# Seven on-chip transposes moved from TensorE to DMA, unread warm-up matmuls, and a new order of loads

## Chip, cores, metric

One core of one Trainium2 chip. The metric is device time in microseconds of one execution, slowest (here only) core; lower is better. A profiled execution also has a span, from its first to its last instruction, which is 1.7 to 2.0 us shorter than that run's time. Ratios are the mean time of one kernel's fast runs over the mean of the other's fast runs of the same rounds, so they are not quite the ratio of the medians quoted beside them. A run more than 1.5% above the fastest of its kernel counts as slow, not fast; medians and ranges below are over all runs, and slow runs are named.

## The reference

Packed attention for 8 batches of 8 heads, then a bilinear feed-forward network; all inputs are random.

```python
p_packed = sm_attn(p, k, v)          # p: 8 x 8 x 32 x 64;  q, k, v: 8 x 8 x 576 x 64
out = sm_attn(q, p_packed, p_packed) # softmax attention, scale 1/8
x = out.transpose(0, 2, 1, 3).reshape(8 * 576, 512)
return ((x @ w1) * (x @ w2)) @ w3 @ w_out   # w1, w2: 512 x 1024; w3: 1024 x 1024; w_out: 1024 x 512
```

## The kernel before

A Python scheduler runs at build time. Each operation has a duration, buffers that it reads and writes, and a wanted time made from tuned constants (`CONF`); a list scheduler with a cost model fixes one order for each engine. On the chip every engine then works through its queue in that order. These parts matter here (cuts marked):

```python
# loads: all on GpSimd's software queue, float32 in HBM cast to float16 on the way;
# two buffers each for k, v and q, used by even and odd batches
def load_in(which, b):
    ...
    env.nc.gpsimd.dma_start(out=t[0:SC, :, :], in_=x[b].rearrange("h (p c) d -> p h (c d)", c=CK))

# a "turn": k or q of one batch, 96 x 3072, transposed on TensorE through PSUM
for g in range(2):
    ps = Psum(2)
    for u in range(2):
        ...   # 6 transposes of 96 x 128 each, 24 in all           (L412)
    ...       # copy PSUM -> kT or qT, on VectorE or ScalarE         (L425, L427)

# va: v is copied into another layout by VectorE                    (L433)
# s1, pv, s2, z: the two attentions (L445, L468, L514, L534)
# fold: w3 @ w_out, once for all (L347 transposes w3, L365 multiplies)
# G: packed values times w1, w2 (L557); gate: a2 times G (L585)
# ab: product of the two gate halves, VectorE, frees the gate's PSUM (L601)
# project: ab times the folded weight (L624); o: copy out; st: store, on SP's queue
```

The softmax here doesn't subtract the row's maximum and nothing guards it: scores larger than these inputs give would overflow.

## Time and profile before

| | before |
|---|---|
| median of the runs beside the changed kernel | 213.82 us (212.99 to 214.01, 4 runs) |
| span of the profiled run | 212.7 us |
| TensorE work, counts times start-to-start durations | 187.9 us |
| TensorE not at work before the turn of q1 | 17.6 us |
| TensorE waiting after it | 1.8 us |
| last matmul's end to the end of the span | 5.3 us |

The turn of q1 is a mark that stands after the same amount of TensorE work, 34.9 us, in both kernels. I got waits by laying the durations that the prediction lists along TensorE's order and subtracting them from the intervals between starts; the prediction, which used rounder numbers, had 2.0 and 5.2 for the last two rows.

### The profile page before, as it was taken

To read this page: it belongs to the slowest core of one execution; us is meant where nothing else is said; L and a number is where in the kernel's file an instruction comes from. 1 tells how busy PE (TensorE), PEld (TensorE's weight loads), DVE (VectorE), ACT (ScalarE), POOL (GpSimd) and SP (SyncE) were. 2 spreads that over 40 slices of the span, in tenths; PEclk is the share of its full clock that TensorE was granted. 3 is DMA by queue.
4 is the path that set the end of the run, shared out by engine and by line. 5 is a ranking of instruction groups with operands and counts; after the bars stand their busy time and mean duration, and the time that the engine had idled before them with its cause. 6 is when DMAs were issued, how large, how long until landed. Compare 5 with 4: busy or idle time off the path is not lost.

```text
span 212.7 us, 6124 instructions
## 1 busy us (share of the span) xinstructions
PE 195.0 (92%) x2656; PEld 131.5 (62%) x2656; DVE 116.0 (55%) x188; ACT 137.0 (64%) x209; POOL 32.9 (15%) x49
## 2 busy tenths in 40 slices
PE   0188989999999999999999999999999999999990
PEld 0168878667567748785457766757755646776440
DVE  4015434367867776587946845447485665555100
ACT  2154749865798476986899555797858567555321
POOL 7742245511131112111000000100000000000000
PEclk9999999999999999999999999999999999999997
DMA  5999999999999999999829203192013313103353
GB/s 68 185 193 202 206 203 200 197 203 204 205 241 230 224 204 249 203 212 205 177 53 150 62 0 103 49 167 80 20 23 82 99 52 99 54 13 86 99 151 101
DMA packets 34124, 29.51 MB, mean 139 GB/s; under 512 B 3888, under 2 KB 28464, under 8 KB 34096
## 3 DMA queue, kind: packets, MB, share of 16 engines
q0 software_dynamic: 28336, 19.66, 62.7%
q1 hardware_dynamic: 5760, 9.44, 15.4%
q8 instruction: 21, 0.34, 0.6%
q14 instruction: 7, 0.06, 0.1%
HBM read 39.32 MB, written 9.44 MB: 229 GB/s over the span
## 4 chain that ended last, share of the span: by engine, by line
PE 89%; DMA 3%; ACT 2%; DVE 2%; issue 1%; POOL 0%; DVEq 0%; ACTq 0%; POOLq 0%
PE ps L585 29%; PE pb L624 29%; PE pb L365 8%; PE ps L412 7%; PE ps L557 5%; DMA ab<-in_moe_w_dram 3%; PE pb L445 2%; PE pb L468 2%; PE ps L534 2%; PE ps L624 2%; PE ps L514 2%; PE pb L347 1%; ACT ab L357 1%; PE ps L445 1%; DVE pT L334 1%
## 5 line engine op out<-in xcount | busy, mean ns | idle before, releaser
L585 PE MATMUL ps<-a,G 128*128 128x288 f16 x512 | 70.8, 286 | 0.2
L624 PE MATMUL pb<-wc,ab 128*128 128x512 bf16 x272 | 68.7, 380 | 0.0
L601 DVE TENSOR_TENSOR ab<-ps,bs 128x576 bf16<-128x576 f32 x64 | 48.2, 755 | 30.7 <-ACT bs L597 25.1
L585 PEld LDWEIGHTS <-G 128*128 128x128 f16 x512 | 48.5, 98 | 17.0 <-issue 0.9
L597 ACT CAST bs<-ps 128x576 bf16<-128x576 f32 x64 | 40.9, 639 | 26.5 <-PE ps L585 26.0
L624 PEld LDWEIGHTS <-ab 128*128 128x128 bf16 x288 | 25.8, 98 | 25.1 <-issue 2.7
L572 ACT CAST G<-ps 128x1024 f16<-128x1024 f32 x20 | 19.8, 1015 | 4.6 <-PE ps L557 4.4
L637 DVE COPY o<-pb 128x512 f32<-128x512 f32 x15 | 10.4, 691 | 20.7 <-PE pb L624 11.0
L639 ACT COPY o<-pb 128x512 f32<-128x512 f32 x19 | 11.1, 585 | 15.3 <-PE pb L624 15.0
L365 PE MATMUL pb<-wo,ab 128*128 128x256 f16 x128 | 16.7, 286 | 2.3 <-ACT ab L357 1.4
L570 DVE CAST G<-ps 128x1024 f16<-128x1024 f32 x12 | 14.4, 1221 | 3.2 <-PE ps L557 2.9
L365 PEld LDWEIGHTS <-ab 128*128 128x128 f16 x128 | 12.5, 102 | 5.2 <-ACT ab L357 2.7
L347 PE MATMUL pb<-ident,ab 128*128 128x128 f16 x48 | 4.8, 266 | 9.0 <-DMA ab<-in_moe_w_dram 9.0
L278 POOL DMA_DIRECT2D qin<-in_q_dram x8 | 6.2, 772 | 40.2 <-PE ps L412 34.2
L427 ACT COPY qT<-ps 128x1152 f16<-128x1152 f16 x9 | 10.0, 1117 | 3.4 <-PE ps L412 3.2
L540 ACT ACTIVATE ln<-ps 128x576 f32<-128x576 f32 x16 | 10.1, 650 | 2.7 <-PE ps L534 2.5
L557 PE MATMUL ps<-w,ppT 64*32 64x256 f16 x512 | 10.9, 272 | 0.1
L544 ACT ACTIVATE ri<-ln 128x576 f16<-128x576 f32 x16 | 10.7, 687 | 0.3
L456 ACT ACTIVATE es<-pb 96x512 f16<-96x512 f32 x18 | 10.4, 594 | 0.6
L347 PEld LDWEIGHTS <-ab 128*128 128x128 f16 x64 | 4.9, 116 | 9.4 <-DMA ab<-in_moe_w_dram 9.0
L357 ACT COPY ab<-pb 128x1024 f16<-128x1024 f16 x5 | 5.0, 1016 | 8.5 <-PE pb L347 8.5
L412 PE MATMUL ps<-ident,kin 96*128 96x96 f16 x192 | 10.3, 206 | 0.0
(56 smaller groups left out, 185.1 us busy)
## 6 DMA issues: line engine op xcount, KB each, us to landing
kin<-in_k_dram POOLq DMA_DIRECT2D x8, 576.0 KB, 13.6
vin<-in_v_dram POOLq DMA_DIRECT2D x8, 576.0 KB, 15.5
qin<-in_q_dram POOLq DMA_DIRECT2D x8, 576.0 KB, 15.5
out_dram<-o SPq DMA_DIRECT2D x24, 192.0 KB, 2.5
out_dram<-o SPq DMA_DIRECT2D x24, 128.0 KB, 2.4
ab<-in_moe_w_dram POOLq DMA_DIRECT2D x8, 256.0 KB, 10.2
w<-in_moe_w_dram POOLq DMA_DIRECT2D x8, 256.0 KB, 12.2
out_dram<-o SPq DMA_DIRECT2D x24, 64.0 KB, 2.2
```

Of the source, the lines that this page charges most:

```text
L347: env.nc.tensor.transpose(t[:, 128 * ct : 128 * ct + 128], env.w3[:, ci, 128 * ct : 128 * ct + 128], env.ident[:, :])
L365: env.nc.tensor.matmul(pv(ps)[:, 0:256], env.w3T[:, ci, 128 * ct : 128 * ct + 128], env.wo[:, h, ct, :], start=(ct == 0), stop=(ct == DFC ...
L412: env.nc.tensor.transpose(t[:, u, SC * hc : SC * hc + SC], s[0:SC, h, 128 * c3 : 128 * c3 + 128], env.ident[0:SC, 0:SC],)
L544: env.nc.scalar.activation(out=env.ri[g][:, :, :], in_=env.ln[g][:, :, :], func=AF.Exp, scale=-1.0)
L557: env.nc.tensor.matmul(pv(ps)[32 * hp : 32 * hp + 32, g, 256 * w : 256 * w + 256], env.ppT[b % 2][64 * g : 64 * g + 64, g, 32 * hp : 32 * ...
L570: env.nc.vector.tensor_copy(o, pv(ps))
L572: env.nc.scalar.copy(out=o, in_=pv(ps))
L585: env.nc.tensor.matmul(pv(ps)[:, half, 0:HS], env.G[b % 2][:, mc // 2, g, w, 128 * (mc % 2) : 128 * (mc % 2) + 128], env.a2[b % 2][:, g, h ...
L597: env.nc.scalar.copy(out=env.bs[bs][:, :, :], in_=pv(ps)[:, :, 0:HS])
L601: env.nc.vector.tensor_mul(env.ab(pair)[:, mc, b % 2, :].rearrange("p (a s) -> p a s", a=2), pv(ps)[:, :, 0:HS], env.bs[bs][:, :, :],)
L624: env.nc.tensor.matmul(pv(ps), ab[:, ic, 128 * t : 128 * t + 128], env.wc[:, ic, :], start=(ic == 0), stop=(ic == DFC - 1),)
L639: env.nc.scalar.copy(out=env.o[ob][:, :], in_=pv(ps))
```

## The change

Its intent: take seven of the sixteen turns off TensorE and give them to the DMA engines' transpose; let loads pause meanwhile (the code's reason for it is "transposes apart from loads"); keep TensorE's clock up from the start with matmuls that nobody reads; and rebuild the scheduler's model of the DMA queue and tune all orders again. Core of the diff:

```diff
 CONF = dict(
-    dma_from=8,
+    turn="q4 q6 k4 k7 q7 q5 k6",
+    order="q3 v2 k4 k2 k3 q4 v5 q5 v4 q2 k5 v3 Tk4 Tq4 Tq5 k7 Tk7 k6 v6 q6 Tk6 Tq6 v7 q7 Tq7",
+    warm=True,
     ...   # all other constants tuned again
-    loads="wo0 w33 w37 w36 pp w30 k_0 w34 wo1 v_0 q_0 w31 w35 k_1 ww0 w32 ww1 ww3 ww2 v_1 q_1",
+    loads="w34 w32 wo0 k_0 w31 w36 w30 pp wo1 k_1 v_0 w33 q_0 w35 w37 ww0 ww1 ww3 ww2 v_1 q_1",
@@ consts: the constant that unread matmuls read is set first
-        nc.vector.memset(env.pT[:, :, :, :], 0.0)
         nc.vector.memset(env.blk[:, :], 0.0)
         ...
+        nc.vector.memset(env.pT[:, :, :, :], 0.0)
@@ attention
-            if by_dma:
+            if f"{which}{b}" in conf["turn"]:
                 def fn(e):
                     ...
-                    env.nc.sync.dma_start_transpose(
+                    return env.nc.sync.dma_start_transpose(
                         out=t[:, 0 : 24 * SC].rearrange("p (j r) -> p j r", j=24),
                         in_=s[0:SC, :, :].rearrange("p h x -> p (h x)"),
                     )
@@ after the plan: loads and transposes wait for each other, group by group
+        op.gates = list(gate_on)
+    def fill(e):
+        for i in range(8):
+            env.nc.tensor.matmul(pv(fill.ps)[:, 0:128], env.blk[:, :], env.blk[:, :], start=True, stop=True)
@@ emission
+        if op.name == "fill":
+            ...
+            for p in getattr(op, "gates", ()):
+                tc.add_manual_dep(made[op].ins, made[p].ins.name, ..., reason="transposes apart from loads")
 (cut: class Dma, the model of the queue, used only to choose the order)
```

More of the change, by code (lines that the diff above doesn't have):

```diff
@@ L22 @@
 CONF = dict(
-    dma_from=8,
-    P=25.15,
-    T0=59.57,
-    lead=1.32,
-    at=dict(kT=-0.8, va=-0.14, s1=0.87, pv=0.59, ppT=-0.87, qT=-0.07, s2=0.43, z=0.51, G=0.14),
-    G_w=-0.01,
-    tg=[-30.99, -12.45, -0.15, 8.05, -11.49, -2.63, 7.81, -7.38, -17.47, 4.27],
-    ta=[-60.59, -5.81, -1.16, 6.18, -17.56, 4.69, -5.65, -11.68],
-    proj_off=0.87,
-    proj_w=0.98,
-    gate_w=0.03,
-    loads="wo0 w33 w37 w36 pp w30 k_0 w34 wo1 v_0 q_0 w31 w35 k_1 ww0 w32 ww1 ww3 ww2 v_1 q_1",
-    fold0=57.8,
-    fold1=3.02,
-    fold_w=3.51,
+    turn="q4 q6 k4 k7 q7 q5 k6",
+    order="q3 v2 k4 k2 k3 q4 v5 q5 v4 q2 k5 v3 Tk4 Tq4 Tq5 k7 Tk7 k6 v6 q6 Tk6 Tq6 v7 q7 Tq7",
+    warm=True,
+    P=29.2291,
+    T0=80.6499,
+    lead=1.3115,
+    at=dict(kT=-1.6236, va=0.0107, s1=0.7618, pv=0.4288, ppT=-1.4299, qT=-1.2631, s2=-1.2122, z=0.5004, G=0.2508),
+    G_w=-0.1978,
+    tg=[-23.1099, -3.311, 10.4569, -2.7587, 6.032, 9.5469, -1.2936, -11.1124, -14.9496, 8.7305],
+    ta=[-46.4062, -60.559, 5.856, -5.9212, -20.778, -0.73, -27.3654, -33.788],
+    proj_off=2.8077,
+    proj_w=1.1912,
+    gate_w=0.0325,
+    loads="w34 w32 wo0 k_0 w31 w36 w30 pp wo1 k_1 v_0 w33 q_0 w35 w37 ww0 ww1 ww3 ww2 v_1 q_1",
+    fold0=107.041,
+    fold1=-16.2447,
+    fold_w=5.6366,
 )
@@ L100, with __init__, run @@
 OVERLAP = {"ACT": 0.10, "DVE": 0.083}
-BEGIN, DMA_BEGIN, LAG = 1.27, 2.6, 0.6
+BEGIN, DMA_BEGIN = 1.27, 2.6
+FILL, FILL_END, WARM_AT = 0.44, 20.0, 6.5
+class Dma:
+    def __init__(self, scale=1.0):
+        self.free, self.scale, self.rest = DMA_BEGIN, scale, 0.0
+    def run(self, t, work):
+        begin = max(self.free, t)
+        work = work * self.scale + (0.3 if self.free == DMA_BEGIN else 1.3 if begin > self.free + 0.5 else 0.0)
+        if begin > self.free + 1.0:
+            self.rest = begin
+        end = begin
+        for a, b, r in ((0.0, 4.4, 1.0), (4.4, 7.2, 0.55), (7.2, 1e9, 1.0)):
+            if end < b and work > 1e-9:
+                step = min(work, (b - max(end, a)) * r)
+                work -= step
+                end = max(end, a) + step / r
+        self.free = end
+        return end + min(0.6 + 0.05 * max(0.0, end - self.rest), 2.6)
 def latency(a, b):
@@ L109, in latency, with schedule @@
     return LATENCY.get((a, b), 0.08)
-def schedule(plan):
+def schedule(plan, warm=CONF["warm"]):
     ops = plan.ops
@@ L118, in schedule @@
     free = {e: BEGIN for e in ("PE", "ACT", "DVE", "POOL", "SP")}
-    free["DMA"] = DMA_BEGIN
+    queue = Dma()
     waiting = {}
@@ L146, in schedule @@
             push(op)
-    order = []
+    order, fills = [], []
     n_left = len(ops)
@@ L180, in schedule @@
         if isinstance(dur, tuple):
-            issue, trans = dur
+            issue, lead, trans = dur
+            done[op], on[op] = queue.run(t + lead, trans), "DMA"
             free[e] = t + issue
-            begin = max(free["DMA"], t + issue + 0.9)
-            if begin < 11.0:
-                trans *= 1.35
-            free["DMA"] = begin + trans
-            done[op], on[op] = begin + trans + LAG, "DMA"
-        else:
-            if e == "PE" and t < 4.0:
+            if e == "SP" and issue > 2:
+                free[e] = max(free[e], queue.free - 0.1)
+        else:
+            cold = e == "PE" and t < (WARM_AT if warm else 15.5)
+            if e == "PE" and warm and FILL_END > t > free[e] + FILL + 0.2:
+                spare = [i for i in range(len(slots) - 1, -1, -1) if slots[i] <= free[e]]
+                n = int((t - free[e] - 0.2) / (FILL * 2 if cold else FILL))
+                if spare and n:
+                    f = Op(op.n, "fill", {"PE": FILL}, plan.fill, 0.0, Psum(1))
+                    f.alloc.at, f.engine, f.repeat = spare[0], "PE", n
+                    start[f], done[f] = free[e], free[e] + n * FILL * (2 if cold else 1)
+                    fills.append(f)
+            if cold:
                 dur *= 2
@@ L204, in schedule @@
                 push(s)
+    order += fills
     order.sort(key=lambda op: (start[op], op.n))
@@ L219, in build_plan, with dma @@
     Ta = [T0 + P * (b - conf["lead"]) + d for b, d in enumerate(conf["ta"])]
-    rate = 0.199e6
-    def dma(nbytes, issue=0.77):
-        return (issue, nbytes / rate)
+    def dma(issue, trans):
+        return (issue, issue + 0.75, trans)
     def pv(p, n=512, dtype=FP32):
@@ L235, in build_plan, with load @@
     seq = [0]
-    def load(name, nbytes, fn, w, r=()):
+    def load(name, cost, fn, w, r=()):
         seq[0] += 1
-        return add("ld " + name, {"POOL": dma(nbytes)}, fn, -1000 + seq[0], w=w, r=r)
+        return add("ld " + name, {"POOL": cost}, fn, -1000 + seq[0], w=w, r=r)
     def load_w3(j):
@@ L243, in fn @@
             env.nc.gpsimd.dma_start(out=env.w3[:, j, :], in_=env.moe_w3[128 * j : 128 * j + 128, :])
-        load(f"w3 {j}", 128 * 1024 * 2, fn, [("w3", j)])
+        load(f"w3 {j}", dma(0.56, 1.25), fn, [("w3", j)])
     def load_wo(h):
@@ L251, in fn @@
             )
-        load(f"wo {h}", 1024 * 256 * 2, fn, [("wo", h)])
+        load(f"wo {h}", dma(1.0, 2.66), fn, [("wo", h)])
     def load_w12(qd):
@@ L260, in fn @@
                 )
-            load(f"w{w + 1} {qd}", 512 * 256 * 2, fn, [("w12", w, qd)])
+            load(f"w{w + 1} {qd}", dma(0.76, 1.34), fn, [("w12", w, qd)])
     def load_p():
@@ L269, in load_p @@
         seq[0] += 1
-        add("ld p", {"POOL": (1.16, 1.46)}, fn, -1000 + seq[0], w=[("pnat",)])
+        add("ld p", {"POOL": dma(1.17, 1.65)}, fn, -1000 + seq[0], w=[("pnat",)])
     def load_in(which, b):
@@ L277, in fn @@
             x = (env.k, env.v, env.q)[src]
-            env.nc.gpsimd.dma_start(
+            return env.nc.gpsimd.dma_start(
                 out=t[0:SC, :, :], in_=x[b].rearrange("h (p c) d -> p h (c d)", c=CK)
             )
-        load(f"{which}{b}", 96 * 3072 * 2, fn, [(which + "in", b % 2)])
+        load(f"{which}{b}", dma(0.78, 2.9), fn, [(which + "in", b % 2)])
     def emit_loads(names):
@@ L387, in attention @@
     def attention(b):
-        by_dma = b >= conf["dma_from"]
         def turned(which):
@@ L401, in fn @@
                     )
-                add(f"{dst} {b}", {"SP": (1.0, 4.0)}, fn, att(b, dst) - 5, r=[(raw, b % 2)], w=keys)
+                add(f"T {which}{b}", {"SP": (2.9, 1.25, 3.2)}, fn, att(b, dst) - 5, r=[(raw, b % 2)], w=keys)
                 return
@@ L521, in fn @@
                         )
-            add(f"s2 {b} {g}", {"PE": 0.15}, fn, att(b, "s2", 0.04 * g), r=[("ppT", b % 2), ("qT", b % 2, 0), ("qT", b % 2, 1)], alloc=ps)
+            add(f"s2 {b} {g}", {"PE": 0.2}, fn, att(b, "s2", 0.04 * g), r=[("ppT", b % 2), ("qT", b % 2, 0), ("qT", b % 2, 1)], alloc=ps)
             def fn(e, g=g, ps=ps):
@@ L648, in fn @@
                     )
-            add(f"st {pair} {t}", {"SP": (0.3, 0.7)}, fn, vt + 0.9 * width / len(tiles), r=[("o", ob)])
+            add(f"st {pair} {t}", {"SP": (0.8, 1.0, 1.0)}, fn, vt + 0.9 * width / len(tiles), r=[("o", ob)])
     def rows_of(t, pair):
@@ L673, in build_plan @@
             project(pair, range(4, 9), Tg[b + 1], P * conf["proj_w"])
+    by_name = {op.name: op for op in plan.ops}
+    names = [("T " if x[0] == "T" else "ld ") + x.lstrip("T") for x in conf["order"].split()]
+    since_load, since_turn = [], []
+    last = None
+    for i, name in enumerate(names):
+        op = by_name[name]
+        if name[0] == "T":
+            if last != "T":
+                since_turn = []
+            gate_on = since_load
+            since_turn.append(op)
+        else:
+            op.vt = i - 500
+            if last == "T":
+                since_load = []
+            gate_on = since_turn
+            since_load.append(op)
+        last = name[0]
+        op.gates = list(gate_on)
+        for p in gate_on:
+            if p not in op.preds:
+                op.preds.add(p)
+                p.succs.append(op)
+    def fill(e):
+        for i in range(8):
+            env.nc.tensor.matmul(pv(fill.ps)[:, 0:128], env.blk[:, :], env.blk[:, :], start=True, stop=True)
+    plan.fill = fill
     return plan
@@ L765 @@
     )
+    made = {}
     for op in order:
-        if op not in first:
-            op.fn(op.engine)
+        if op.name == "fill":
+            op.fn.ps = op.alloc
+            for _ in range(op.repeat):
+                op.fn(op.engine)
+        elif op not in first:
+            made[op] = op.fn(op.engine)
+            for p in getattr(op, "gates", ()):
+                tc.add_manual_dep(
+                    made[op].ins,
+                    made[p].ins.name,
+                    mybir.DependencyInfo(mybir.DependencyClass.Sync, mybir.DependencyReason.DATA),
+                    reason="transposes apart from loads",
+                )
 _INS = ['q', 'k', 'v', 'p', 'moe_w1', 'moe_w2', 'moe_w3', 'moe_w_out']
```

## The prediction

> **What bounds the kernel now.** I read the page's list of engines first, then the chain of work that ended last, then the timeline of TensorE and the DMA view. Parts 1 and 4 of the page of the kernel before:
>
> ```profile
> PE 195.0 (92%) x2656; PEld 131.5 (62%) x2656; DVE 116.0 (55%) x188; ACT 137.0 (64%) x209; POOL 32.9 (15%) x49
> ...
> PE 89%; DMA 3%; ACT 2%; DVE 2%; issue 1%; POOL 0%; DVEq 0%; ACTq 0%; POOLq 0%
> ```
>
> TensorE (PE) is busy for 92% of the span and makes 89% of the chain; VectorE and ScalarE are far from full. But "busy" counts overlapping matmuls, so I count TensorE in start-to-start time, which the chain in order of time gives, because there the pieces do not overlap:
>
> ```profile
> 2.27 6.70 DMA ab<-in_moe_w_dram
> 9.02 1.05 PE pb L347 x8
> ...
> 11.16 1.89 PE pb L365 x8
> ...
> 110.07 1.02 PE ps L412 x24
> 111.09 0.86 PE pb L624 x4
> 111.96 0.98 PE ps L585 x8
> ```
>
> The reader sees three things. Nothing runs on TensorE until 9.0 us, when the first quarter-megabyte of w3 lands. The first matmuls are slow: 236 ns for each of eight L365 matmuls at 11 us, where the timeline has 48 of them in 5.41 us (113 ns) at 23 us. And turning one k or q of one batch (24 transposes at L412) costs 1.02 us of the chain, wedged between projections and gates: it is on the path, one for one.
>
> Per matmul, from such pieces: L585 122.5 ns, L624 216, L365 109, L412 42.5, L557 21, L445 29, L514 23, L534 122.5, L468 10.4 (four run side by side), 128-column transposes 56. Times their counts this is 187.9 us of TensorE work. Laid along the order of the program, 23.0 us stand before the first gate matmul and 34.9 us before the turn of q1 (first batch counted as 0). The timeline of TensorE has these two at:
>
> ```profile
> 39.17 0.67 PE L585 MATMUL ps<-a,G 128*128 128x288 f16 x4
> ...
> 52.55 0.93 PE L412 MATMUL ps<-ident,qin 96*128 96x96 f16 x18
> ```
>
> So up to 52.55 us TensorE lost 52.55 - 9.02 - 34.9 = 8.6 us (about 3 of it slow clock, the rest waits), and after it nearly nothing: 187.9 - 34.9 = 153.0 us of work until its end at 207.5 us, so 2.0 us of waits. The last copies and stores take 5.2 us more (to 212.7).
>
> Two stages, then: a ramp fed by loads, and a long stage that TensorE alone sets. In the ramp DMA runs at its rate without pause. Stretches of 5 us:
>
> ```profile
> 0.00:5.00 5.00, 0.00 (x0) 0.00 (x0) 2.47 (x10) 1.28 (x1) 3.87 (x11) 1.00 0.49 60
> ...
> 15.00:20.00 5.00, 4.33 (x47) 3.76 (x48) 2.13 (x4) 2.62 (x4) 2.01 (x3) 1.00 1.33 202
> 20.00:25.00 5.00, 4.74 (x78) 4.22 (x77) 1.93 (x4) 3.98 (x7) 0.54 (x1) 1.00 1.32 204
> ```
>
> The last column, about 203 GB/s, holds to 50 us. Weights, p and k, v, q of batches 0 and 1 are 9.05 MB as 16-bit values, so the last of them, q1, lands at about 3 + 45 + 2 = 50 us. The turn of q1 at 52.55 is only about 2 us after that. This is what caps any gain in the ramp.
>
> **What the Trainium skill says.** "TensorE: Matmul & The Clock Gate", Part 1, has an idle array at 1.2 GHz and a warm one at 2.4 GHz after about 3.4 us of sustained work, with N/1.2 GHz or N/2.4 GHz + 2.5 ns from start to start. The trace agrees: for 256 columns that is 213 and 109 ns, against the 236 (with one fill of the pipeline) and 113 above; for 96 columns 42.5 ns, as measured. So matmuls nobody reads can warm the array before the first load lands. "DMA: Bandwidth & Descriptors", Latency and other measured facts, gives a DMA transpose 261 GB/s with a non-contiguous middle dimension; "Advanced Engine Details and Errata", X-Bar Transpose (TRN2), says transposes are as fast as regular DMAs. The trace of before holds no DMA transpose, so neither is tested; 590 KB at 261 GB/s would be 2.3 us, at this kernel's 203 GB/s 2.9 us (an estimate). "DMA: Bandwidth & Descriptors", Anatomy of one DMA, puts the fixed cost of a software-queue DMA near 2.0 us. This trace differs: a k load issued alone at 111.3 us took
>
> ```profile
> kin<-in_k_dram POOLq DMA_DIRECT2D x1, 576.0 KB, 8.2
> ```
>
> 8.2 us from issue to landing, 2.9 of which is data at 203 GB/s. I use 8 us for the first load after a pause.
>
> **The change part by part.**
>
> *Transposes off TensorE.* Seven turns go: 7 x 24 matmuls x 42.5 ns = 7.1 us, leaving 180.8. All seven lie after 52.55 us, in the stage without slack, so the whole 7.1 us should come off. Fourteen copies out of PSUM (7 x 2, about 0.75 us on VectorE or 1.12 on ScalarE) go as well; those engines aren't the bound, so I count nothing.
>
> *Warm start and a new load order.* The built program puts 32 unread matmuls ahead of everything and 80 more in the first waits, and loads w3 first instead of half of w_out. Real work can start near 6 us instead of 9, at full clock. Both are worth up to 6 us in themselves, but TensorE works in order and the turn of q1 still stands after 34.9 us of work and after q1's landing at about 50. From 6 us there are 44 us for 34.9 us of work, so loads set that moment: I take 51.3, a gain of 1.3 us. Four to five of the six are hidden.
>
> *Load pauses.* Three groups of transposes on SP's queue: k4, q4, q5; then k7; then k6, q6 (and q7 last). Loads wait for transposes and the reverse. I give a transpose 5.5 us alone (2.9 + issue and receipt) and 3.5 more for each next one. With TensorE at time W + 17 for work W laid along its order: q5 lands about 86, the group is done about 99 and k4 is needed at 97, after that q4 at 103 and q5 at 117. k7 must wait for batch 5's scores to free the buffer (113), is done at 119, needed at 128. Then k6, v6, q6 (8 + 2 x 2.9) land at 133, k6 is turned by 139 and needed at 141; q6 by 142, needed at 147; v7 by 150, needed at 154; q7 by 158, needed at 163. Nothing should miss by much, but slack is 2 to 6 us and once negative. I put waits after q1 at 3.0 us, against 2.0 before.
>
> *The queue model* costs nothing itself; it only chooses orders.
>
> *Sum.* 51.3 + (180.8 - 34.9) + 3.0 = 200.2 for TensorE's end, + 5.2 = 205.4 span; the timed median stood 1.2 us above the span (213.93 against 212.7), so **206.7 us**.
>
> **The rivals.** *A, a transpose or the loads behind it come late.* If a transpose takes 8 us rather than 5.5, or runs on few DMA engines, or a pause stretches, k4 and k6 come late; the in-order TensorE and, behind the transposes in SP's queue, the output stores stop too. For it: slack of a few us, software loads that take 8 us after a pause. Against: DMA is a fifth to a third busy after 120 us, and three or four output tiles of buffer stand behind a blocked store. It would give back 3 to 10 us: 209 to 216. *B, the ramp is worth more.* If load order and warm clock get q1's batch and the first gate done earlier than I think, and waits stay at 2 us, up to 3 us more: 203 to 204. Against it: the bytes and rate of DMA do not change. *C, another engine becomes the bound.* ScalarE at 64% and VectorE at 55% lose copies rather than gain them; I give this little, 1 us at most.
>
> **Range and chances.** B's end and A's mild form make 203.5 to 210.5. A 2% gain needs 209.65, which leaves A 3 us of lateness beyond my estimate; I give faster 0.87, within 2% 0.11, slower 0.02.
>
> **What would show it right or wrong.** Right: L412 down from 384 to 216 matmuls; the first real matmul at 5 to 7 us, L365 near 110 ns from the outset; the turn of q1 at 50.5 to 52.5 and not at 46; TensorE's waits after it 2 to 4 us; the end of TensorE near 200. Wrong on pauses: waits of TensorE at L445 or L514 for a DMA into kT or qT, or of copies for the output stores, longer than 2 us each. Wrong on the ramp: q1's turn before 50 us. Wrong altogether: a transpose that takes well over 6 us, or matmuls after 52 us that cost more from start to start than before.

## More of the kernel before

TensorE writes gate products to three pairs of PSUM banks; a pair is free again when ScalarE (`bs`) or VectorE (`ab`) has read it. So a VectorE queue that stands still stops TensorE soon after.

## The result, and the profile after

The changed kernel takes 207.71 us (median; 207.31 to 209.06, 4 runs) against 213.82 us. The ratio is 0.9732, 95% interval 0.9681 to 0.9784: faster by 2.7%. In a later session the same kernel gave 208.76 us (206.85 to 211.06, 6 runs) against 213.51 (213.23 to 213.96), ratio 0.9761. The run of 211.06 counts as slow; the five fast ones still spread over 2.4 us, where the 11 runs of the kernel before stay within 0.8. That scatter turns out to be a clue, though a weak one: in a third session 25 fast runs of the kernel before spread over 2.5 us too.

The page of the changed kernel, its first line and the two on DMA queues (line numbers have moved: 412 is now 441, 445 is 474, 585 is 614, 601 is 630, 624 is 653):

```profile
PE 194.7 (94%) x2600; PEld 130.3 (63%) x2600; DVE 110.1 (53%) x180; ACT 130.3 (63%) x203; POOL 33.0 (16%) x49
...
q0 software_dynamic: 28336, 19.66, 64.8%
q1 hardware_dynamic: 22112, 13.57, 27.2%
```

TensorE has 56 matmuls fewer: 168 transposes gone and 112 unread ones added. Its busy time hardly moves, for the unread ones count as busy. The hardware queue carries 4.1 MB more than the stores' 9.44 MB, which is seven transposes of 590 KB.

All instructions of the transposing line, and when SP issued them (start, duration, what; the duration is the time in SP's queue, in the first view its least, middle and greatest value in ns):

```profile
L427 SPq DMA_TRANSPOSE qT<-qin x4: 2775/3006/3185, 95.4 to 159.0; - x4
L427 SPq DMA_TRANSPOSE kT<-kin x3: 3113/3397/3507, 91.7 to 137.7; - x3
...
DMA to landing us min/median/max: 4.7/5.0/6.6
```

```profile
91.74 3.51 SPq L427 DMA_TRANSPOSE kT<-kin  x1
95.35 6.05 SPq L427 DMA_TRANSPOSE qT<-qin  x2
...
115.78 3.40 SPq L427 DMA_TRANSPOSE kT<-kin  x1
```

A transpose lands 5.0 us after its issue (median) and the next of a group follows 3.0 to 3.6 us later. The prediction had 5.5 and 3.5. At 590 KB every 3.0 us a transpose moves 196 GB/s (worked out), near the 203 GB/s of the loads and under the 261 that the prediction quotes.

The same count of TensorE's time as before gives the table (us; last two columns are from experiments below, so that they can be compared):

| | before | after | before, turns dropped | two pauses |
|---|---|---|---|---|
| TensorE work | 187.9 | 180.8 | 180.8 | 180.8 |
| not at work before q1's turn | 17.6 | 17.2 | 17.3 | 16.7 |
| waits after it | 1.8 | 3.6 | 5.5 | 3.3 |
| TensorE ends | 207.4 | 201.6 | 203.6 | 200.7 |
| rest of the span | 5.3 | 4.5 | 4.4 | 4.5 |
| span | 212.7 | 206.0 | 208.0 | 205.2 |

So of 6.7 us of span, 7.1 come from the turns, 0.5 from the ramp and 0.9 from the end of the last stores, and 1.8 are given back as waits after q1's turn. The 0.9 us are no gain of the change: the profiled run of the kernel before took 214.42 us, 0.6 above the median of the table, and the same kernel with its turns dropped has 4.4 us there, like all others. Where the waits stand, the chain of work of the changed kernel shows. First near 64 us, then near 135:

```profile
43.01 21.06 DMA qin<-in_q_dram
...
64.12 0.68 PE ps L441 x12
...
68.66 0.76 DVE ab L630
...
115.78 6.65 DMA kT<-kin
...
123.86 10.18 DMA vin<-in_v_dram
134.04 0.02 issue
134.07 0.04 DVE va L462
...
134.94 0.76 DVE ab L630
```

At 64 us TensorE waits for the load of q2 and loses 0.4 us; at 68.7 us (the `ab` of VectorE) it loses 0.8 us, because VectorE's copy of v3 stood before that `ab` in the queue and waited for its load until 67.8 us. Neither has to do with the pauses. At 135 us the chain is longer: the third load group (k6, v6, q6) had to wait until k7's transpose had landed at 122.4; v6 was then 10.2 us on its way; VectorE's copy of it (L462) stood at the head of VectorE's queue; the gate products behind it came late; and TensorE, out of PSUM, waited. The timeline shows VectorE and TensorE there (in brackets the idle time before, and what ended it):

```profile
134.07 0.96 DVE L462 COPY va<-vin 96x3072 f16<-96x3072 f16 x1 [2.29 <-DMA vin<-in_v_dram]
...
134.94 2.31 DVE L630 TENSOR_TENSOR ab<-ps,bs 128x576 bf16<-128x576 f32 x3
...
135.74 1.80 PE L614 MATMUL ps<-a,G 128*128 128x288 f16 x12 [0.30 <-DVE ab L630]
```

TensorE first reads the copy of v6 at 146.8 us (L497), 12 us later. The copy hurts only because the queue is strictly in order, as the Trainium skill has it ("TensorE: Matmul & The Clock Gate", Architectural detail: ACT and DVE are strict FIFO); this trace agrees, with three gate products issued back to back once the copy had gone.

In start-to-start time TensorE loses 0.5 us here. In the repeat of the same kernel, v6 landed later and VectorE stood for 3.8 us:

```profile
134.99 0.96 DVE L462 COPY va<-vin 96x3072 f16<-96x3072 f16 x1 [3.76 <-DMA vin<-in_v_dram]
...
136.66 1.56 PE L614 MATMUL ps<-a,G 128*128 128x288 f16 x10 [1.77 <-DVE ab L630]
```

and TensorE lost 1.9 us instead of 0.5.

### The profile page after: what moved, and what is told of

Its sections match the earlier page's. It is cut to its first block, busy times and chain, and to the rows that moved or that the text cites.

```text
span 206.0 us, 6019 instructions
## 1 busy us (share of the span) xinstructions
PE 194.7 (94%) x2600; PEld 130.3 (63%) x2600; DVE 110.1 (53%) x180; ACT 130.3 (63%) x203; POOL 33.0 (16%) x49
## 3 DMA queue, kind: packets, MB, share of 16 engines
HBM read 39.32 MB, written 9.44 MB: 237 GB/s over the span
## 4 chain that ended last, share of the span: by engine, by line
PE 57%; DMA 36%; issue 2%; POOL 2%; DVE 1%; ACT 0%; POOLq 0%; DVEq 0%
PE pb L653 23%; PE ps L614 22%; DMA qin<-in_q_dram 10%; DMA ab<-in_moe_w_dram 8%; DMA w<-in_moe_w_dram 6%; DMA vin<-in_v_dram 5%; DMA kin<-in_k_dram 5%; DMA kT<-kin 3%; PE ps L586 3%; PE ps L653 2%; PE ps L441 2%; PE ps L563 1%; PE pb L474 1%; PE ps L543 1%; PE pb L497 1%
## 5 line engine op out<-in xcount | busy, mean ns | idle before, releaser
L653 PE MATMUL pb<-wc,ab 128*128 128x512 bf16 x272 | 67.8, 380 | 0.0
L614 PEld LDWEIGHTS <-G 128*128 128x128 f16 x512 | 48.4, 98 | 19.3 <-issue 3.2
L601 ACT CAST G<-ps 128x1024 f16<-128x1024 f32 x19 | 18.6, 1016 | 2.6 <-PE ps L586 2.6
L599 DVE CAST G<-ps 128x1024 f16<-128x1024 f32 x13 | 15.8, 1223 | 3.8 <-PE ps L586 3.8
L396 PE MATMUL pb<-wo,ab 128*128 128x256 f16 x120 | 14.8, 273 | 1.6 <-DMA wo<-in_moe_w_out_dram 1.0
L309 POOL DMA_DIRECT2D kin<-in_k_dram x8 | 6.2, 779 | 55.6 <-PE ps L614 29.0
L396 PEld LDWEIGHTS <-ab 128*128 128x128 f16 x128 | 11.9, 98 | 3.9 <-issue 0.9
L554 ACT ACTIVATE es<-ps 128x576 f16<-128x576 f32 x16 | 9.9, 652 | 4.7 <-PE ps L543 4.5
L454 DVE COPY kT<-ps 128x1152 f16<-128x1152 f16 x6 | 4.4, 752 | 14.1 <-PE ps L441 14.1
L309 POOL DMA_DIRECT2D vin<-in_v_dram x8 | 6.2, 774 | 34.7 <-DVE ppn L511 23.0
L410 ACT CAST wc<-pb 128x256 bf16<-128x256 f32 x10 | 3.7, 373 | 9.7 <-PE pb L396 9.1
L577 DVE TENSOR_TENSOR a<-es,ri 128x576 f16<-128x576 f16 x16 | 7.2, 453 | 4.7 <-ACT ri L573 4.4
## 6 DMA issues: line engine op xcount, KB each, us to landing
w<-in_moe_w_dram POOLq DMA_DIRECT2D x8, 256.0 KB, 11.6
```

What stands on the lines that cost most here:

```text
L309: return env.nc.gpsimd.dma_start(out=t[0:SC, :, :], in_=x[b].rearrange("h (p c) d -> p h (c d)", c=CK))
L396: env.nc.tensor.matmul(pv(ps)[:, 0:256], env.w3T[:, ci, 128 * ct : 128 * ct + 128], env.wo[:, h, ct, :], start=(ct == 0), stop=(ct == DFC ...
L599: env.nc.vector.tensor_copy(o, pv(ps))
L601: env.nc.scalar.copy(out=o, in_=pv(ps))
L614: env.nc.tensor.matmul(pv(ps)[:, half, 0:HS], env.G[b % 2][:, mc // 2, g, w, 128 * (mc % 2) : 128 * (mc % 2) + 128], env.a2[b % 2][:, g, h ...
L653: env.nc.tensor.matmul(pv(ps), ab[:, ic, 128 * t : 128 * t + 128], env.wc[:, ic, :], start=(ic == 0), stop=(ic == DFC - 1),)
```

## The experiments

My theory before them: TensorE's bound makes the seven turns worth their 7.1 us; the ramp gives almost nothing, since loads set it; the pauses cost what v6's lateness costs. Rival A: pauses, and stores stuck behind transposes, eat several microseconds. Rival B: the warm start is worth what it saves on paper. A third rival: without pauses it would be worse.

**The changed kernel again**, as the base for the three beside it.

> The changed kernel once more, unedited, as the base for the three kernels that run beside it. Every theory expects 0.97 of the kernel before (about 207.5 us).

Measured: the 208.76 us above, 0.9761 of the kernel before (0.9730 to 0.9791); the scatter was not expected.

**Unread matmuls left out** of the changed kernel, all else in place.

```diff
         if op.name == "fill":
-            op.fn.ps = op.alloc
-            for _ in range(op.repeat):
-                op.fn(op.engine)
+            continue
```

> The changed kernel with its 112 unread matmuls left out and every other instruction in its place. My theory (the ramp is set by the landing of loads, the saved slow clock becomes waiting): slower by 0 to 1.0 us than the changed kernel, with L396 near 236 ns from start to start at 10 us instead of 109. Rival B (the warm clock is worth what it saves on paper): slower by 2.5 to 3.5 us.

Measured: 209.14 us (207.11 to 211.24, of which the last counts as slow), ratio 0.9773 against 0.9761 for the changed kernel beside it, so slower by 0.1%, well inside the intervals (each about 0.3% to either side). TensorE's timeline, without them and then with them:

```profile
5.12 1.03 PE L378 MATMUL pb<-ident,ab 128*128 128x128 f16 x8 [5.12 <-DMA ab<-in_moe_w_dram]
...
10.55 3.57 PE L396 MATMUL pb<-wo,ab 128*128 128x256 f16 x16 [2.94 <-DMA wo<-in_moe_w_out_dram]
13.92 2.12 PE L441 MATMUL ps<-ident,kin 96*128 96x96 f16 x24
...
19.03 1.04 PE L396 MATMUL pb<-wo,ab 128*128 128x256 f16 x8
...
29.39 0.61 PE L378 MATMUL ps<-ident,ab 128*128 128x128 f16 x8
```

```profile
10.01 1.91 PE L396 MATMUL pb<-wo,ab 128*128 128x256 f16 x16 [0.55 <-DMA wo<-in_moe_w_out_dram]
...
13.71 1.19 PE L441 MATMUL ps<-ident,kin 96*128 96x96 f16 x24 [0.90 <-DMA kin<-in_k_dram]
...
17.85 1.04 PE L396 MATMUL pb<-wo,ab 128*128 128x256 f16 x8
...
29.46 0.62 PE L378 MATMUL ps<-ident,ab 128*128 128x128 f16 x8 [0.73 <-DMA ab<-in_moe_w_dram]
```

The clock effect is all there: sixteen L396 take 3.57 us cold and 1.91 warm (213 and 109 ns from start to start). With it the changed kernel comes to the same eight L396 1.2 us earlier, at 17.85 us instead of 19.03. But it then waits longer for loads: for the second half of w_out at 21.5 us (the lead shrinks to 0.6 to 0.9 us) and 0.73 us for a part of w3 at 29.46 us, where the kernel without the matmuls, which came later, waits for nothing. From there the two stand at the same place within 0.1 us, until past q1's turn. Rival B falls.

**The same matmuls put into the kernel before**: 100 of them while TensorE has nothing to do.

```diff
         nc.vector.memset(env.blk...)        # moved ahead of the memset of pT
     for op in order:
         if op not in first:
             op.fn(op.engine)
+            if op.name == "consts":
+                for _ in range(100):
+                    nc.tensor.matmul(env.singles[1][:, 0:128], env.blk[:, :], env.blk[:, :], start=True, stop=True)
```

> The kernel BEFORE with 100 unread matmuls in TensorE's first 9 us (and the constant they read set first), nothing else changed. My theory: the saved slow clock (about 3 us) mostly becomes waiting for loads, so faster by 0 to 1.5 us, with q1's turn at 51 to 52.5 us. Rival B: faster by 2.5 us or more.

Measured: 214.30 us (214.01 to 214.53, 20 runs) against 213.47, ratio 1.0027 (1.0011 to 1.0043): slower by 0.3%, outside my expectation by a little. In the profiled run the ramp did gain: q1's turn at 51.14 us instead of 52.55. That lead of 1.4 us held until 67 us and fell to 0.2 or 0.3 us here:

```profile
67.80 0.96 DVE L433 COPY va<-vin 96x3072 f16<-96x3072 f16 x1 [1.55 <-DMA vin<-in_v_dram]
...
69.48 0.65 PE L585 MATMUL ps<-a,G 128*128 128x288 f16 x4 [0.92 <-DVE ab L601]
```

v3 lands at 67.8 us, where it lands in the changed kernel too (its copy starts at 67.78 there), and again a copy at the head of VectorE's queue stops TensorE. A second loss, 1.3 us near 100 us, is a pause inside a group of equal matmuls for which the profile shows no cause; without it TensorE would not have ended later than in the kernel before in this profile.

**Seven turns dropped from the kernel before**, nothing in their place; wrong (the comparison with the reference passes all the same: it is too loose to see stale q and k, so "correct" says little for this kernel's attention).

```diff
+    gone = ("kT 4", "kT 6", "kT 7", "qT 4", "qT 5", "qT 6", "qT 7", "kTc 4", "kTc 6", "kTc 7", "qTc 4", "qTc 5", "qTc 6", "qTc 7")
     for op in order:
-        if op not in first:
+        if op not in first and op.name[: op.name.find(" ") + 2] not in gone:
             op.fn(op.engine)
```

> The kernel BEFORE with the turns of k4, k6, k7, q4, q5, q6, q7 (TensorE transposes and their copies out of PSUM) left out and nothing put in their place; every other instruction stays where it was and the result is wrong on purpose. It is the first part of the change alone, with no pause to pay. My theory (TensorE is the bound, each turn counts 1.02 us): faster than the kernel before by 6.6 to 7.4 us, so about 206.5. Rival (waits of other engines take the place of some turns): by 3 to 6 us.

Measured: 209.61 us (209.25 to 209.91) against 213.47, ratio 0.9808: faster by 3.9 us, half of what I expected, and at the lower end of the rival's. TensorE's work fell by 7.1 us as counted, but its waits after q1's turn rose from 1.8 to 5.5 us. The chain of this run, cut to pieces that are not TensorE, shows the largest of them:

```profile
100.73 1.23 issue
...
109.81 0.68 ACT ri L544
110.49 0.55 ACT ln L540
...
141.54 0.55 ACT ln L540
...
142.12 0.69 ACT ri L544
...
142.83 0.47 DVE a L548
```

The chain of a batch's second softmax (exponential, sum, logarithm, reciprocal, product: ScalarE and VectorE in turn) used to run while TensorE did turns and other work; near 143 us the chain of the kernel before has two groups of turns in this place:

```profile
142.15 1.02 PE ps L412 x24
...
144.28 1.53 PE ps L412 x36
```

In the old order TensorE now reaches the first gate matmul before the product is ready. Counted from start to start, the waits at softmax chains that stand out (over 0.25 us; near 110, 140 and 142 us) make 1.7 us of the 3.7 added. The pause near 100.7 us makes 1.4 us and is again without a cause in the profile; whether the old order has to do with it is not shown. So the turns are not worth their duration with the order left as it was.

**All transposes dropped from the changed kernel**, with the waits of loads for them (wrong as well).

```diff
+        if op.name.startswith("T "):
+            continue
```

> The changed kernel with its seven DMA transposes and the waits of loads for them left out; the result is wrong on purpose, since old k and q are used. It shows what the pauses cost. My theory: the transposes are hidden but for the late load of v6 (0.6 us of TensorE waiting near 135 us), so faster than the changed kernel by 0.3 to 1.2 us. Rival A (pauses, and stores held up behind the transposes, eat part of the gain): faster by 2 to 4 us.

Measured: 206.87 us (206.44 to 207.39), ratio 0.9681, against 208.76 and 0.9761 beside it. The transposes and pauses thus cost 0.8%, 1.7 us, in that session (by the intervals 1.0 to 2.4), more than my 1.2 at the middle and short of rival A's 2; the runs do not decide between the two. The scatter is smaller too: 0.95 us from lowest to highest, instead of 2.4 in the fast runs of the changed kernel. And TensorE's wait near 135 us is gone. Laid beside the profile of the repeat, matmul by matmul, TensorE is 0.6 us behind at q2's turn and 1.5 us ahead from 138 us to the end: that wait makes the whole difference of the two spans (1.6 us). Against the kernel before with its turns dropped (209.61, another session), where no transposes are done either, it is 2.7 us faster: that is what order, load order and unread matmuls bring together. The matmuls alone bring 0.1%, so the orders bring the rest; which of them was not separated.

**Each transpose issued twice** (right result).

```diff
             made[op] = op.fn(op.engine)
+            if op.name.startswith("T "):
+                made[op] = op.fn(op.engine)
```

> The changed kernel with each DMA transpose issued twice in a row (the same data, the result stays right). It takes the slack away. My theory: the chain from the third pause on has 2 to 6 us of slack and seven more transposes put some 18 us into it, so k6 and v6 come some 10 us late: slower by 8 to 15 us. Rival (DMA is half idle after 100 us, so transposes have ample room): slower by under 2 us.

Measured: 234.39 us, ratio 1.0945: slower by about 25 us than the changed kernel, well over my range. I had missed that the second of a pair writes the same tile and so waits for the first to land: each pair costs two whole landings of 5 us. Lateness then reaches TensorE in every group. Its longest waits after the ramp (in us: total, times, longest):

```profile
PE ps L614 <- DVE ab L630: 6.6, 2, 6.0
PE ps L497 <- DVE va L462: 5.0, 1, 5.0
PE pb L474 <- DMA kT<-kin: 4.0, 2, 2.1
PE ps L543 <- DMA qT<-qin: 3.7, 2, 1.9
```

It shows that there is no ample room, and that late v copies did more harm here (11.6 us) than late k and q (7.7). A long wait also costs more than itself:

```profile
149.19 3.04 PE L614 MATMUL ps<-a,G 128*128 128x288 f16 x12 [5.98 <-DVE ab L630]
```

After this wait the gate products started 240 ns apart, and so again after the wait of 5.0 us, instead of 122.5; the granted clock was 0.62 from 150 to 155 us and 0.55 from 180 to 185. The waits listed are 19.3 us of the 25; slow matmuls make much of the rest.

**No waits between loads and transposes** (data dependencies stay).

```diff
-            for p in getattr(op, "gates", ()):
+            for p in ():
```

> The changed kernel with the waits between loads and transposes dropped (data dependencies stay; the order in each queue stays). My theory: the pauses are what makes v6 late; without them the late loads come 10 us or more earlier, so faster than the changed kernel by 0.5 to 2 us and less scattered, even if a transpose beside loads takes up to twice as long. The writer's theory, which is the rival: a transpose beside loads is slowed so much (landing 10 us and more) that k4 or q4 come late: slower by 2 us or more.

Measured: 211.05 us (208.54 to 216.32, 6 runs), ratio 0.9833 (0.9788 to 0.9877), against 0.9691 for the next kernel in the same session and 0.9732 and 0.9761 for the changed kernel in others: slower than the changed kernel by 1.5 to 2.2 us. Two runs, 211.88 and 216.32, count as slow; the fast ones spread over 2.5 us, hardly more than the changed kernel's. My theory fell here. Transposes beside loads land late, and k4 is late for its scores:

```profile
DMA to landing us min/median/max: 5.2/9.0/11.5
```

```profile
100.43 0.41 PE L474 MATMUL pb<-pT,kT 128*128 128x64 f16 x8 [1.76 <-DMA kT<-kin]
```

A pause of 0.9 us at 110.7 us, once more without a cause in the profile, adds to it.

**Two pauses instead of three**: k6, v6 and q6 loaded before k7's transpose.

```diff
+    move("ld k6", "ld k7"); move("ld v6", "ld k6"); move("ld q6", "ld v6")    # each after the other
+    for x in ("ld k6", "ld v6", "ld q6"):
+        named[x].gates = [named[y] for y in ("T k4", "T q4", "T q5")]
+    named["T k7"].gates = [named[y] for y in ("ld k7", "ld k6", "ld v6", "ld q6")]
```

> The changed kernel with the loads of k6, v6, q6 moved ahead of the transpose of k7 (they wait for the first group of transposes only, and k7's transpose waits for them): one pause fewer, nothing else moved. My theory: v6's copy no longer stops VectorE near 135 us, so TensorE's wait there (0.5 to 1.9 us) goes: faster than the changed kernel by 0.4 to 1.9 us, less scattered. Rival (the scatter and the waits come from the transposes themselves): no difference.

Measured: 207.06 us (206.98 to 207.13), ratio 0.9691. As expected: under the changed kernel by 0.9 to 1.5 us (0.9691, interval 0.9666 to 0.9716, against 0.9732 and 0.9761 in its two sessions; only the second stands clear of it, and the two kernels never ran side by side), and a scatter of 0.15 us. The profile bears it out, for VectorE no longer waits for v6:

```profile
131.49 0.95 DVE L462 COPY va<-vin 96x3072 f16<-96x3072 f16 x1
```

The transposes landed after 5.0 us (median) as before, so the middle pause had bought nothing. k7's transpose has to wait for batch 5's scores to free its buffer until 115 us, while GpSimd's queue stood idle from 104 us with k6, v6 and q6 behind that transpose.

**v3's copy later in VectorE's queue**, on top of two pauses.

```diff
+    move("va 3", "ab 1 3"); move("ld v5", "va 3")
```

> The kernel of two_pauses, and VectorE's copy of v3 (with the load of v5, which needs its buffer) placed three gate products later in VectorE's queue. My theory: v3 lands at 67.7 us in every kernel and its copy, which nobody needs before 75 us, stops VectorE's queue and so TensorE for 0.75 us; that wait goes: faster than two_pauses by 0.5 to 0.9 us. Rival (the PE wait has another cause, or q3's landing takes its place): no difference.

Measured: 206.88 us (206.62 to 207.06), ratio 0.9682 against 0.9691: the fastest correct kernel, by 0.1%, which the intervals do not separate. The wait for v3's copy is gone and the rival that I had named took its place, two microseconds on:

```profile
63.93 0.68 PE L441 MATMUL ps<-ident,qin 96*128 96x96 f16 x12 [0.64 <-DMA qin<-in_q_dram]
...
70.45 0.68 PE L441 MATMUL ps<-ident,qin 96*128 96x96 f16 x12 [0.48 <-DMA qin<-in_q_dram]
```

Now q3's load ends the wait. So loads still set the pace when q3 lands at 70.4 us, well after q1's turn; the gains tried before that point became the next wait for a load.

**Loads of q2 and v2 exchanged**, and the same without unread matmuls.

```diff
+    move("ld v2", "ld q2"); move("va 2", "qTc 2 0")
```

> The kernel best, with the loads of q2 and v2 exchanged and v2's copy put after q2's. My theory: q2's turn, which waits 0.4 to 0.8 us for its load at 63 us, gets it 3 us earlier: faster than best by 0.4 to 0.8 us. Rival (v2 now comes late for the product that needs it at 66.5 us): the same or slower.

> The kernel best2 without its unread matmuls. My theory: with later load waits out of the way a gain of the ramp can now get through, so the matmuls may be worth up to 0.8 us here where they were worth 0.1 % before. If the first load's landing alone sets the ramp: no difference within 0.3 us.

Measured: both WRONG (relative error 0.47) and 222 us. The fault is mine: the copy of v2 was moved behind the load of v4, which takes the same buffer, so it read v4. In a framework that derives waits from program order, such a move changes the meaning without a race. The profile of `best2` shows it: VectorE stood 14.6 us at that copy, waiting for a load, and TensorE 14.7. The times say nothing of the exchange, and whether q2's wait can be had is open.

**The old load order with the new rest**, unread matmuls at most 96 at a time.

```diff
-    loads="w34 w32 wo0 k_0 ...",
+    loads="wo0 w33 w37 w36 pp w30 k_0 w34 ...",   # as before
```

> The kernel best with the load order of the kernel before for the first 21 loads; the scheduler reorders the rest, and the unread matmuls are at most 96 at a time. In the kernel before with unread matmuls the first gate matmul came at 37.7 us and q1's turn at 51.1, against 40.4 and 52.1 in the changed kernel, so the new load order looks worse in the ramp. My theory: q1's turn about 1 us earlier, and 0 to 1 us faster than best. Rival (the orders that the search found belong together): slower by 1 us or more.

Measured: 209.59 us (209.52 to 210.21), ratio 0.9816: 2.7 us slower than the kernel it was made from. The first gate matmul does come earlier, at 38.0 us, but q1's turn still at 52.1, and new waits for k and q loads follow (1.0 us before 64.9 and 1.1 us before 71.4). Orders and loads were tuned together; one alone is no test of the other, so whether the new load order is better in itself stays open.

## Why the prediction was right

It said 206.7 us, 203.5 to 210.5, faster by over 2% with 0.87; measured were 207.71 us and 2.7%. Step by step:

- *Seven turns off TensorE are 7.1 us.* The count is right: L441 is down to 216 matmuls and TensorE's work by 7.1 us. "On the path, one for one" was too simple: with the turns dropped and the old order kept only 3.9 us were gained, in part because softmax chains came out from under them. The change's new orders, for which the prediction had no term, made up the difference (2.7 us between the two kernels without these turns); that the sum came out was some luck.
- *Warm start and load order, together 1.3 us at q1's turn.* Measured 0.5 us in the profile after, and 1.0 to 1.2 us in the profiles of three kernels with the same ramp (q1's turn at 51.57, 51.32 and 51.31). The reason, loads hide the rest, is shown by leaving the matmuls out (0.1%) and by adding them to the old kernel (no gain). But the cap that I drew at q1's landing sits elsewhere: no profile shows TensorE waiting for q1 at its turn, and the waits stand before it (part of w3 at 29.5 us) and after it (q2 at 64, v3 at 67.7 and q3 at 70.4 us).
- *Pauses: waits after q1 of 3.0 us instead of 2.0.* Measured 3.6 instead of 1.8, and 5.3 in the repeat. Only 0.5 us (1.9 in the repeat) of this stands at 135 us and comes from the pauses; the waits for q2 and v3, 1.2 us, belong to the ramp's loads. The durations of the transposes were right. I put the tight spots at k4 and k6, waited for by TensorE; k4 was in time, and the wait came by another road, v6 to VectorE's queue to PSUM to TensorE, which my list of dates did not hold: it had v6's landing (133 us; its copy began at 134.1), but not that VectorE would stand at the copy from 131.8 us on. Rival A in a mild form is what happened: 1.7 us and most of the scatter, by lateness of loads. Stores were held up too: behind the transposes of k6 and q6, VectorE waited 2.0 us for an output buffer at 146.4 us, as it never does without transposes, but TensorE lost nothing that stands out there.
- *Tail 5.2 us and 1.2 us from span to time.* They were 4.5 and 1.7; the two errors nearly cancel. Both come from one slip: the span of one run, which took 214.42 us and had long last stores, was set against the median of other runs, 213.93. Its own difference was 1.7.
- *ScalarE and VectorE don't become the bound* (rival C): right for their share of busy time (63% and 53%), but VectorE's order mattered twice.

One reading of the prediction needs a word: its 236 ns for a cold L365 counts the modelled end of the last matmul; from start to start the trace has 213 ns.

Not settled: the pauses inside equal matmuls, 1.1 and 1.2 us near 100 us in two variants of the kernel before and 0.9 us at 110.7 us without the waits. All three begin 0.2 to 0.6 us after the end of a 16 KB transfer on DMA queue q8, which the profile labels "instruction"; some 20 such transfers stand in each profile, and no other is followed by a pause like this. Whether they are the cause is not shown.

## What to carry to other kernels

Work taken off the bounding engine pays in full only where that engine has other work ready (3.9 of 7.1 us here with the old order); look for the chains on other engines that the removed work covered, and order again. A load that lands late hurts most where its consumer stands at the head of an in-order queue whose later work frees buffers for the bound engine: move such copies back, or load earlier. Before speeding up a start, find the last load that sets the pace, not the first: gains ahead of it turn into waits at it.

## What the Trainium skill lacked or had wrong

- "DMA: Bandwidth & Descriptors", Latency and other measured facts, gives 261 GB/s for a DMA transpose. Here a 590 KB transpose, SBUF to SBUF, lands 5.0 us after issue (median, 4.7 to 6.6) and the next one follows 3.0 us later within a group, which is 196 GB/s if that interval is the transfer (worked out, not measured as a rate).
- The same page, Rules for kernel authors, says that a transpose next to ordinary DMAs needs nothing. For results that held (the kernel without pauses was correct); for time it did not: landing went from 5.0 to 9.0 us (median), and the kernel was 1.5 to 2.2 us slower. A word on keeping the two apart in time is lacking.
- The same page, Anatomy of one DMA, has 2.0 us of fixed cost and bytes / 436 GB/s, so 3.4 us for the 590 KB that a casting load writes, or 4.7 us for the 1,180 KB of float32 that it reads (both worked out from it). Such a load, alone in its queue but beside stores, took 8.2 us, and 7.5 us another time (6.0 us at the least in the changed kernel); about 203 GB/s, counted by the bytes written, was the rate in a full queue. What a cast costs is on none of the pages that I read.
- "TensorE: Matmul & The Clock Gate", Part 1, was right: 107 ns for 128 columns from start to start before warming (32 unread matmuls in 3.41 us), and for 256 columns 213 ns cold and 109 warm. It does not say that loads can hide the whole gain of an early warm-up (0.1% here).
- No page that I read names the case met twice here: an engine's in-order queue held by a copy that waits for a load, which stops TensorE through PSUM (0.5 to 1.9 us each time where the result was right).
